# Projections of an adaLN and infini-attention block: x transposed ahead of the kernel, modulation columns on VectorE, and memory in groups of seven heads

## The chip, the cores and the metric

The kernel runs on one core of a Trainium2 chip. The metric is the device time of one execution in microseconds (us). Of the kernel before there are three timed runs, of 1843.55, 1843.55 and 1844.84 us, median 1843.55 us, and one more run that was profiled.

A core has four compute engines with a list of instructions each: TensorE (PE in the profile, its weight loads are PEld), VectorE (DVE), ScalarE (ACT) and GpSimd (POOL). SyncE (SP) issues most DMAs, in the order of its list. Matrix products go to PSUM banks of 128 x 512 floats; everything else lives in SBUF tiles of 128 partitions or in DRAM.

## The reference

One token stream of 2048 tokens and 576 features goes through an attention block and a feed-forward block, both with a modulated layer norm. The attention works on four segments of 512 tokens with 32 heads of 18, and carries a linear memory from segment to segment.

```python
mod = (silu(c) @ w_mod).reshape(1, 6, 1, 576)
sa, ca, ga, sb, cb, gb = (mod[:, i] for i in range(6))
h = layernorm(x) * (1 + ca) + sa
q, k, v = h @ wq, h @ wk, h @ wv                # 32 heads of 18, 4 segments of 512
phi = lambda t: where(t > 0, t + 1, exp(t))
for s in range(4):                              # M and z start at 0
    a_dot = softmax(qs @ ks.T * scale + causal) @ vs
    a_mem = (phi(qs) @ M) / (phi(qs) @ z + 1e-6)
    o_s = sigmoid(beta) * a_mem + (1 - sigmoid(beta)) * a_dot
    M, z = M + phi(ks).T @ vs, z + phi(ks).sum(tokens)
x = x + ga * (o @ wo)
h = layernorm(x) * (1 + cb) + sb
x = x + gb * ((silu(h @ w_gate) * (h @ w_up)) @ w_down)
```

## The kernel before

All products are done at about float32 precision: an operand is split into a rounded high part and a remainder, and a product takes three matmuls (high by high, low by high, high by low). So each operand comes as a pair: hh and hl for the normalised x, wqkh and wqkl for the weights of q and k, fh and fl for a projected tile.

**Projections, 0 to 242 us.** `wk1`, `ps1` and other pools hold this stage, in which the scheduler of the tile framework orders the instructions of each engine by what they depend on and by the order of the code. A loop runs over the four segments s. In each, `proj(s, t)` makes nine tiles of 128 features x 512 tokens (t 0 to 4 hold k, 4 to 8 hold q), each by 14 matmuls of 512 columns (tile pp); `vproj(s, i)` makes v for four groups of 128 tokens, two halves of 14 matmuls with 288 columns (pv); `phi_k` transposes a k tile (ptk) and forms phi(k) (pk); and `mem(s)` multiplies pk with v into five memory tiles (pm), which VectorE masks into mbd and GpSimd adds to the segment before. Results are stored to DRAM by SyncE: kD and qD hold three rows a feature (high, high, low for k, and high, low, high for q), since the scores are later made from stacks of these rows.

The input of a segment is made by `prep` and `trans_in`. `prep(s + 1)` loads x, takes mean and variance on VectorE and normalises it there. `trans_in(s + 1)` then lets TensorE transpose it, five groups of four 128 x 128 transposes (tile pt), and ScalarE and VectorE scale, shift and split each group into hh and hl. The groups stand at the end of a segment, between the last pv matmuls and the memory tiles: the border.

The modulation vectors: those of the first layer norm are made at the start (tiles wm, pr, row, pcr, colv). The four others follow in `late_mod`, from segment 1 on: products of w_mod rows with silu(c) are summed on VectorE (macc), and summed over partitions by TensorE, either into rows for the two gates (`mod_row`) or into columns for the second layer norm (`mod_col`: 20 matmuls of one column each, twice).

PSUM has eight banks. In this stage three belong to pp and pv, two to pt and ptk (tag t), one to memory and modulation (tag m), and two to scores (tag s1). `early()` runs the first pass of the first two attention units during the segments 1 to 3: scores s and their row maxima, `E1` steps a projection tile and `E2` steps a pv group.

**Attention, 242 to 613 us.** Here the order is written out by hand. There are 32 units of four heads of one segment, each in 11 steps. `PAT` names the events of each step by letters: among them A0, A1 and B0, B1, C (num, phi(q) by memory, in two halves, its copies and its division), M0 to M3 and X (output projection of attention: pw, from oh and ol), R, S, T, Z (its transposes of o), m and n (row maxima transposed), and g, h (phi of q). `RL` sets the steps of another stream, which prepares the feed-forward input.

**Feed-forward, 613 us to the end**, follows and is not changed.

Memory before: head groups of 128 feature rows don't fall on head limits (18 rows a head), so `mem` and `num_a` take one tile of 76 columns and four of 152 (eight heads with 19 columns each), the heads at the limits stand in two tiles, and `num_c` adds the halves. 

Of the kernel before, what the change touches and what calls it, by code (L numbers as in the profile page):

```python
# [15 lines left out]
P = 128  # L16
S = 2048
# [14 lines left out]
MB = [0, 3, 10, 17, 24]  # L32
MO = [0, 76, 228, 380, 532]
# [29 lines left out]
E1 = 3  # L63
E2 = 2
BK = 0
PAT = (["E", "", "U D", "m c", "n G", "Q d", "M0", "g M1 M2 M3 X", "h A0", "R S q T Y Z B0", "A1 f P z B1 C"],
# [3 lines left out]
LNA = 1  # L70
RB = 9
RL = (-6, -1, 0, 4, 4, 10, 11, 11, 13, 11, 12, 13, 16, 17)
# [9 lines left out]
def block(ctx: ExitStack, tc: tile.TileContext, x, wqk, wv, wo, beta, wgu, wgr, wd, c, w_mod, w_mod0, w_mod1, out):  # L82
# [8 lines left out]
    def chain(*g):  # L91
        for a in g:
            yield from a

# [57 lines left out]
    kD = [dr.tile([D, 3, L], F32, tag=f"kD{s}", name=f"kD{s}") for s in range(NSEG)]  # L152
# [3 lines left out]
    xhD = [dr.tile([P, 4, D], F32, tag=f"xh{s}", name=f"xh{s}") for s in range(NSEG)]  # L156
    xD = [dr.tile([P, 4, D], F32, tag=f"xD{s}", name=f"xD{s}") for s in range(NSEG)]
# [6 lines left out]
    mbd = vst.tile([P, 3, 5, 152], F32, tag="mbd", name="mbd")  # L164
# [4 lines left out]
    SB = [2]  # L169

    def load_stack(u, b):
        s, q = units[u]
        k, v = [d[s].rearrange("f z t -> (f z) t").rearrange("(Q a r) t -> Q r a t", Q=8, a=2)[q] for d in (kD, qD)]
        for r0, r1 in ((0, 96), (96, 108)):
            nc.sync.dma_start(f32(kst[b][r0:r1]), k[r0:r1])
        for r0, r1 in ((0, 48), (54, 102), (48, 54), (102, 108)):
            nc.sync.dma_start(f32(qst[b][r0:r1, r0 // 54:4:2, :]), v[r0:r1])
# [6 lines left out]
    def p1_step(u, b, i, ps, jp, jb):  # L184
# [18 lines left out]
        if i == 0:  # L203
            nc.gpsimd.tensor_scalar(mc[:, 0], mx, -1.0, 0.0, op0=ALU.mult, op1=ALU.add)
            lo = mwk.tile([P, 4, 4], F32, tag="ml", name="ml")
            nc.gpsimd.tensor_tensor(lo, mx, f32(mc[:, 0]), op=ALU.add)
            nc.gpsimd.tensor_scalar(mc[:, 1], lo, -1.0, 0.0, op0=ALU.mult, op1=ALU.add)
# [35 lines left out]
    def transpose_group(pt, src, kt):  # L243
        for i in range(4):
            n = P if kt < 4 else 64
            nc.tensor.transpose(pt[:n, 128 * i:128 * i + 128], src(i)[:, 128 * kt:128 * kt + n], ident)
# [10 lines left out]
    with ExitStack() as p1:  # L257
# [8 lines left out]
        def early():  # L266
            for u in range(2):
                load_stack(u, u)
            for u in range(NE):
                yield from p1_unit(u, u, ps, "m", 1, pb, 2)  # L270
# [6 lines left out]
        bdm = w1.tile([P, 5, 8, VW], F32, tag="bdm", name="bdm")  # L277
        nc.gpsimd.memset(bdm, 1.0)
        for t in range(5):
            off = 128 * t - 64 - DH * MB[t]  # L280
            nc.gpsimd.affine_select(out=bdm[:, t], in_=bdm[:, t], pattern=[[-DH, 8], [0, VW]], compare_op=ALU.is_ge,
                                    fill=0.0, base=off, channel_multiplier=1)
            nc.gpsimd.affine_select(out=bdm[:, t], in_=bdm[:, t], pattern=[[DH, 8], [0, VW]], compare_op=ALU.is_ge,
                                    fill=0.0, base=DH - 1 - off, channel_multiplier=-1)
# [6 lines left out]
        def load_x(s):  # L291
            t = xs[s] = x1.tile([P, 4, D], F32, tag="x", name=f"x{s}")
# [22 lines left out]
        def mod_col(a, slot, add):  # L315
            pc = ps.tile([P, L], F32, tag="m", name="pc", bufs=1)
            for c in range(6):
                c0 = 288 * (c // 3) + 128 * (c % 3)
                if c % 3 < 2:
                    nc.tensor.matmul(pc[:, c:c + 1], lhsT=a[:, c0:c0 + 128], rhs=ones[0:96, 0:1], start=True, stop=True)  # L320
# [1409 lines left out]
```

## Time and profile before

| what | us |
|---|---|
| median of the three timed runs | 1843.55 |
| the profiled execution's own time | 1842.27 |
| its span in the trace | 1840.5 |
| TensorE busy | 1806.1 |
| VectorE busy | 1488.5 |
| ScalarE busy | 1095.0 |
| GpSimd busy | 642.1 |
| 243 to 613 us: TensorE busy of 370 | 356.3 |
| 613 us to the end: TensorE busy of 1227.5 | 1221.2 |

The profile comes from one execution that the hardware profiler recorded. Its span leaves out 1.8 us around the recorded work. In rows of groups, "idle before" is what the engine waited ahead of these instructions, and the name behind the arrow is what ended most of it. In rows of the timeline, the first number is the start and the second the length; TensorE overlaps its instructions, so a length is more than the distance to the next start. A matmul on 32-bit data shows as two instructions.

### The profile page before, as it was taken

What the parts mean: (1) busy time and instruction counts of PE and PEld (TensorE: products, weight loads), DVE (VectorE), ACT (ScalarE), POOL (GpSimd) and SP (SyncE); (2) the same over time, 40 slices, a digit from 0 to 9 for tenths busy, and PEclk for the clock granted to TensorE, in tenths of its full rate; (3) what the DMA queues carried; (4) which work ended last, traced back from release to release, by engine and by line L of the source; (5) the groups of instructions that cost most, each with busy time, mean ns of one, the idle gap of its engine ahead of it and who ended that gap; (6) DMA issues with size and microseconds to landing.
All of it is one profiled execution on the core that took longest, in us unless ns stands there. A gap on an engine that the chain in (4) does not pass through costs nothing.

```text
span 1840.5 us, 31635 instructions
## 1 busy us (share of the span) xinstructions
PE 1806.1 (98%) x10727; PEld 1535.0 (83%) x10727; DVE 1488.5 (81%) x3361; ACT 1095.0 (59%) x2380; POOL 642.1 (35%) x1118
## 2 busy tenths in 40 slices
PE   7999999999999999999999999999999999999999
PEld 4888866787776888888888888898888888888888
DVE  7455358878886799898898899868888888888886
ACT  3333468878776567777777777634454544544541
POOL 5000058776556575565665665400000000000000
PEclk9999999999999999999999999999999999999999
DMA  7767677778674845555545545485332333334331
GB/s 262 226 229 258 234 208 193 201 203 210 177 183 145 289 145 188 162 160 174 161 156 177 147 135 160 153 292 169 128 106 84 122 106 111 102 100 128 106 101 53
DMA packets 149417, 305.56 MB, mean 166 GB/s; under 512 B 30057, under 2 KB 60905, under 8 KB 147337
## 3 DMA queue, kind: packets, MB, share of 16 engines
q1 hardware_dynamic: 138360, 259.20, 48.0%
q10 hardware_dynamic: 10896, 44.36, 6.2%
q8 instruction: 85, 1.39, 0.3%
q14 instruction: 76, 0.61, 0.1%
HBM read 193.29 MB, written 109.64 MB: 165 GB/s over the span
## 4 chain that ended last, share of the span: by engine, by line
PE 90%; DVE 3%; DMA 3%; ACT 2%; POOL 1%; issue 1%; SPq 0%; ACTq 0%; POOLq 0%; DVEq 0%
PE A L1258 25%; PE pd L1377 19%; PE C L1258 12%; PE B L1258 6%; PE pp L108 5%; PE av L651 4%; PE s L194 3%; PE pv L108 3%; PE pw L761 3%; PE s L627 3%; PE pd L1397 3%; DVE junk L199 1%; ACT Pt L634 1%; PE pm L458 1%; PE pn L832 1%
## 5 line engine op out<-in xcount | busy, mean ns | idle before, releaser
L1258 PE MATMUL A<-y,wh 128*128 128x512 f32 x1152 | 404.2, 391 | 2.5 <-ACT B L1304 1.8
L1385 DVE TENSOR_TENSOR acc<-acc,pd 128x576 f32<-128x576 f32 x327 | 245.4, 751 | 77.2 <-PE pd L1377 71.4
L199 DVE CUSTOM_DVE_ANT_0 junk<-s,tri 128x256 bf16<-128x256 f32 (+3 forms) x512 | 221.8, 484 | 64.9 <-PE s L194 49.7
L1377 PE MATMUL pd<-dh,ah 128*128 128x288 f32 x896 | 267.4, 298 | 0.1
L1377 PE MATMUL pd<-dl,ah 128*128 128x288 f32 x896 | 263.8, 294 | 0.0
L1377 PE MATMUL pd<-dh,al 128*128 128x288 f32 x896 | 262.4, 293 | 0.0
L1258 PEld LDWEIGHTS A<-y,wh 128*128 128x128 f32 x1152 | 216.2, 188 | 41.3 <-ACT B L1304 2.1
L1220 DVE TENSOR_TENSOR wl<-O,wh 128x256 fp32r<-128x256 f32 x504 | 241.9, 483 | 3.5 <-ACT wh L1219 2.9
L1258 PE MATMUL A<-y,wl 128*128 128x512 f32 x576 | 224.6, 390 | 0.0
L634 ACT ACTIVATE Pt<-s 128x512 f32<-128x512 f32 (+1 forms) x352 | 181.6, 559 | 48.2 <-PE s L627 28.3
L1258 PE MATMUL C<-y,wh 128*128 128x512 f32 x576 | 202.7, 393 | 0.0
L1219 ACT CAST wh<-O 128x256 fp32r<-128x256 f32 x504 | 198.2, 405 | 2.8 <-DMA O<-in_wgu_dram 1.5
L1377 PEld LDWEIGHTS pd<-dh,ah 128*128 128x128 f32 x896 | 168.1, 188 | 19.0 <-ACT pd L1353 4.1
L1323 DVE TENSOR_TENSOR al<-sg,ah 128x512 fp32r<-128x512 f32 x240 | 178.3, 743 | 6.6 <-ACT ah L1322 6.5
L1377 PEld LDWEIGHTS pd<-dl,ah 128*128 128x128 f32 x896 | 169.5, 189 | 16.2
L1213 POOL TENSOR_TENSOR O<-O 128x128 f32<-128x128 f32 x280 | 155.4, 588 | 64.7 <-DMA O<-in_wgu_dram 27.7
L1377 PEld LDWEIGHTS pd<-dh,al 128*128 128x128 f32 x896 | 169.1, 189 | 0.0
L1322 ACT CAST ah<-sg 128x512 fp32r<-128x512 f32 x240 | 149.2, 621 | 26.3 <-DVE sg L1282 24.8
L627 PE MATMUL s<-qs,ks 110*128 110x512 f32 (+2 forms) x384 | 143.8, 392 | 5.3 <-ACT Pt L634 4.1
L194 PE MATMUL s<-ks,qs 108*128 108x256 f32 (+3 forms) x512 | 144.3, 334 | 2.1 <-DVE mx L199 1.9
L1258 PEld LDWEIGHTS C<-y,wh 128*128 128x128 f32 x576 | 108.0, 188 | 18.8
L1258 PEld LDWEIGHTS A<-y,wl 128*128 128x128 f32 x576 | 108.2, 188 | 14.8
(377 smaller groups left out, 4084.5 us busy)
## 6 DMA issues: line engine op xcount, KB each, us to landing
wr<-rD SPq DMA_DIRECT2D x216, 112.0 KB
O<-in_wgu_dram SPq DMA_DIRECT2D x36, 512.0 KB
oD<-O ACTq DMA_DIRECT2D x36, 512.0 KB
O<-oD SPq DMA_DIRECT2D x36, 512.0 KB
O<-in_wgu_dram SPq DMA_DIRECT2D x36, 384.0 KB
ks<-kD SPq DMA_DIRECT2D x32, 384.0 KB
qs<-qD SPq DMA_DIRECT2D x64, 192.0 KB
y<-yD SPq DMA_DIRECT2D x11, 1024.0 KB
```

The costliest lines, as they stand in the source:

```text
L194: nc.tensor.matmul(bank[:, n * (h - h0):n * (h - h0) + n], lhsT=qst[b][0:108, h, 128 * i:128 * i + 128], rhs=kst[b][0:108, h // 2, 0:n], s ...
L199: nc.vector.tensor_tensor_reduce(junk[:, :n], bank[:, n * (h - h0):n * (h - h0) + n], tri[:, L - n:], 1.0, -3e38, op0=ALU.add, op1=ALU.max ...
L627: nc.tensor.matmul(bank[:, n * (g - h):n * (g - h + w)].rearrange("p (a b) -> p a b", a=w), lhsT=kst[u % NB][0:110, g // 2, 128 * j:128 * ...
L634: nc.scalar.activation(pt[:, h:h + per, :n], bank[:, :n * per].rearrange("p (a b) -> p a b", a=per), AF.Exp, scale=SCALE)
L1213: eng.tensor_tensor(o[:, d, i, s_], o[:, a, i, s_], o[:, b, i, s_], op=op)
L1219: nc.scalar.copy(wh, o)
L1220: later.append(lambda: nc.vector.tensor_tensor(wl, o, f32(wh), op=ALU.subtract))
L1258: nc.tensor.matmul(bank, lhsT=a, rhs=b, start=(first and n == 0), stop=(n == 6), skip_group_check=not first)
L1322: nc.scalar.copy(ah, src)
L1323: later.append(lambda: nc.vector.tensor_tensor(al, src, f32(ah), op=ALU.subtract))
L1377: nc.tensor.matmul(pd[:, i, :288], lhsT=a[:, tk], rhs=w, start=(add and k == 0), stop=(k == 2), skip_group_check=not add)
L1385: nc.vector.tensor_tensor(o, o, pd[:, :, :288], op=ALU.add)
```

## The change

- **x transposed.** The host also passes x transposed (`xt`). For the segments 1 to 3, `prep` loads it as five tiles of 128 features x 512 tokens, and loads the rows of x as well, only for mean and variance. GpSimd forms the reciprocal deviation; mean and deviation go to DRAM (sD) and come back broadcast to all partitions (two tiles rw). GpSimd then subtracts, multiplies and scales each tile, and `cast_in` at the border casts it on ScalarE (hh) and subtracts on VectorE (hl). Segment 0 keeps its transposes.
- **Modulation columns on VectorE.** `mod_col` goes. Nine products with a sum, of 128 x 576, take its place on VectorE, with silu(c) broadcast to all partitions (srow, a reciprocal of 128 x 576 among its steps). `late_mod` starts in segment 2 instead of late in segment 1.
- **Seven-head memory groups.** Memory tiles hold seven heads, 126 rows and 133 columns, four times, and one of four heads, 72 x 76. No head stands in two tiles, and `num_c` adds nothing. The tag m goes: memory and `mod_row` use the two banks of tag t, pr and pcr those of s1.
- **Three store buffers.** fh and fl become one tile with three buffers; kD holds high and low once; a k tile is stored by one DMA instead of two, and the stack of k is loaded by three DMAs, the high row twice.
- **A fixed first order.** The matmuls of pr, the first two groups of pt and pcr are pinned to the order of the code.
- **A third bank for first-pass scores**, with two `early` steps a projection tile and one a pv group instead of three and two. The small steps that end a first pass move from GpSimd to VectorE for the first two units.
- wv's high part is cast on ScalarE instead of GpSimd, and a few events of `PAT` and `RL` stand a step earlier.

```diff
-E1 = 3
-E2 = 2
+E1 = 2
+E2 = 1
-       ["U E", "", "D m", "n", "G c", "d", "M0 M1 M2 M3 X Q g h", "R S", "q A0 B0 T", "Z Y", "P f z A1 B1 C"],
-       ["D E", "U m l", "n G p", "M0", "M1 M2 M3 X A0", "B0", "x c", "d", "", "A1 Q g", "B1 q Y h C P f"])
+       ["U E", "", "D m", "n", "G c", "M0 d", "M1 M2 M3 X Q g h", "R S T", "A0 B0", "q Z Y", "P f z A1 B1 C"],
+       ["D E", "U m l n", "G p", "M0 M1", "M2 M3 X", "A0", "x c B0", "d", "", "A1 Q g", "B1 q Y h C P f"])
...
-    SB = [2]
+    SB = [3]
...
         def late_mod():
+            pk_ = [("r", 2, k) for k in range(6)] + [("c", n) for n in range(9)] + [("r", 5, k) for k in range(6)]
...
+            nc.scalar.activation(se, srow, AF.Exp, scale=-1.0)
+            nc.vector.tensor_scalar(se, se, 1.0, None, op0=ALU.add)
+            nc.vector.reciprocal(se, se)
+            nc.vector.tensor_tensor(srow, srow, se, op=ALU.mult)
...
+                    nc.vector.tensor_tensor_reduce(t, t, srow, 1.0, 1.0 if b < 4 else 0.0, op0=ALU.mult, op1=ALU.add,
+                                                   accum_out=d)
...
+        def cast_in(s):
+            hh, hl, hr = new_h(s)
+            for kt in range(5):
...
+                    nc.scalar.copy(hh[kt], f)
+                    nc.vector.tensor_tensor(hl[kt], f, f32(hh[kt]), op=ALU.subtract)
...
         def prep(s):
+            load(0)
+            load(1)
+            nc.sync.dma_start(t[:, 0:4], xt[0:512, L * s:L * s + L].rearrange("(k p) t -> p k t", p=P))
+            nc.sync.dma_start(t[0:64, 4], xt[512:576, L * s:L * s + L])
...
+            nc.gpsimd.tensor_tensor(mr[:, 1], mr[:, 1], mhalf[:, :4], op=ALU.pow)
+            nc.sync.dma_start(sD[s].rearrange("z (p i) -> p z i", i=4), mr)
+            for z in range(2):
+                nc.sync.dma_start(rw[z], sD[s][z].partition_broadcast(P))
...
+            for kt in range(5):
+                n = P if kt < 4 else 64
+                f = t[:n, kt]
+                nc.gpsimd.tensor_tensor(f, f, rw[0][:n], op=ALU.subtract)
+                nc.gpsimd.tensor_tensor(f, f, rw[1][:n], op=ALU.mult)
+                nc.gpsimd.tensor_scalar(f, f, colv[:n, kt, 0:1], colv[:n, kt, 1:2], op0=ALU.mult, op1=ALU.add)
...
         def mem(s):
             for t in range(5):
-                nh = 4 if t == 0 else 8
-                n = nh * VW
-                pm = ps.tile([P, L], F32, tag="m", name="pm", bufs=1)
+                n, r = NH[t] * VW, NH[t] * DH
+                pm = ps.tile([P, L], F32, tag="t", name="pm")
                 for i in range(4):
-                    nc.tensor.matmul(pm[:, :n], lhsT=pk[:, i, 128 * t:128 * t + 128],
-                                     rhs=vs[s][:, i, VW * MB[t]:VW * MB[t] + n], start=(i == 0), stop=(i == 3))
+                    nc.tensor.matmul(pm[:r, :n], lhsT=pk[:, i, PR * t:PR * t + r],
+                                     rhs=vs[s][:, i, 7 * VW * t:7 * VW * t + n], start=(i == 0), stop=(i == 3))
...
+            fb = pb.tile([P, 2, L], F32R, tag="fh", name="fh", bufs=3)
...
-            tg = trans_in(s + 1) if s + 1 < NSEG else iter(())
             for i in range(4):
...
-                if i == 2:
-                    next(tg, None)
+            tg = cast_in(s + 1) if s + 1 < NSEG else iter(())
             next(tg, None)
             if s < 3:
                 for _ in mem(s):
                     next(tg, None)
```

Three places of the program show how instructions move. First, TensorE's list at the border between segments 0 and 1, before; pv, pm and pp are the tiles named above, pt a transpose group, s a first-pass score:

```order
L108 MATMUL pv<-wvl,hr 128x288
L246 MATMUL pt<-ident,x_603 128x128 x4
L458 MATMUL pm<-vs_728,pk 128x76 x4
L246 MATMUL pt<-ident,x_603 128x128 x4
L458 MATMUL pm<-vs_728,pk 128x152 x4
L108 MATMUL pp<-hh_827,wqkh 128x512
L108 MATMUL pp<-hh_827,wqkl 128x512
L108 MATMUL pp<-hl_831,wqkh 128x512
L458 MATMUL pm<-vs_728,pk 128x152 x4
```

The same place with the change:

```order
L113 MATMUL pv<-wvl,hr 128x288
L534 MATMUL pm<-vs_732,pk 126x133 x16
L534 MATMUL pm<-vs_732,pk 72x76 x4
L113 MATMUL pp<-hh_864,wqkh 128x512
L113 MATMUL pp<-hh_864,wqkl 128x512
L113 MATMUL pp<-hl_868,wqkh 128x512
```

The transposes are gone, and the five memory tiles, which were spread among transposes and the first matmuls of the next segment, stand in one run right behind the last pv. 

Second, the start of TensorE's list, before (pr sums the modulation of the first layer norm, pt transposes segment 0's x, pcr turns the row into columns):

```order
L371 MATMUL pr<-wm_252,sgb 32x320 x4
L246 MATMUL pt<-ident,x_248 128x128 x4
L371 MATMUL pr<-wm_255,sgb 32x320 x4
L246 MATMUL pt<-ident,x_248 128x128
L371 MATMUL pr<-wm_258,sgb 32x320 x4
L246 MATMUL pt<-ident,x_248 128x128 x3
L378 MATMUL pcr<-ident,row 128x128 x2
L378 MATMUL pcr<-ident,row 64x128
L475 MATMUL pp<-hh_354,wqkh 128x512
```

The same place with the change:

```order
L373 MATMUL pr<-wm_248,sgb 32x320 x4
L255 MATMUL pt<-ident,x_244 128x128 x4
L373 MATMUL pr<-wm_251,sgb 32x320 x4
L373 MATMUL pr<-wm_254,sgb 32x320 x4
L380 MATMUL pcr<-ident,row 128x128 x2
L380 MATMUL pcr<-ident,row 64x128
L255 MATMUL pt<-ident,x_244 128x128 x4
L551 MATMUL pp<-hh_359,wqkh 128x512
```

Both lists have eight transposes here. Before, the first four belonged to the first two groups, two each, and took the x tiles that were ready first; now they are the whole first group, ahead of the last two parts of pr, and the second group stands behind pcr. 

Third, SyncE's list in segment 0, from the last k stores on, before (wvraw are the loads of wv, x those of the next segment):

```order
L497 DMA kD_94<-fh 64x2x512
L498 DMA kD_94<-fl 64x512
L503 DMA qD_90<-fh 64x2x512
L504 DMA qD_90<-fl 64x512
L539 DMA wvraw<-in_wv_dram 128x576
L295 DMA x_603<-in_x_dram 128x576 x2
L503 DMA qD_90<-fh 128x2x512
```

The same place with the change:

```order
L572 DMA kD_94<-fh 128x1024
L504 DMA sD_125<-mr 128x2x4
L577 DMA qD_90<-fh 64x512
L572 DMA kD_94<-fh 64x1024
L506 DMA rw<-sD_125 128x512 x2
L576 DMA qD_90<-fh 64x1024
L612 DMA wvraw<-in_wv_dram 128x576 x2
L576 DMA qD_90<-fh 128x1024
```

The loads of the next x have moved ahead of this piece, the store of mean and deviation and its two broadcast loads have come in, and two loads of wv, instead of one, now stand here, behind them.

More of the change, by code (lines that the diff above doesn't have):

```diff
@@ L93, in chain, with once @@
             yield from a
+    def once(g):
+        yield next(g)
     def run(g):
@@ L269, in early @@
             for u in range(NE):
-                yield from p1_unit(u, u, ps, "m", 1, pb, 2)
+                yield from p1_unit(u, u, ps, "t", 2, pb, 2)
             load_stack(2, 2)
@@ L539, in load_wv @@
                 nc.sync.dma_start(r, wv[:, k, :])
-                split(wvh[:, k], wvl[:, k], r)
+                nc.scalar.copy(wvh[:, k], r)
+                nc.vector.tensor_tensor(wvl[:, k], r, f32(wvh[:, k]), op=ALU.subtract)
                 yield
@@ L593, in block @@
                     next(tg, None)
-            for _ in tg:
-                pass
+            run(tg)
         run(ge)
```

287 lines of the change are left out of this document (157 added, 130 removed).

## Prediction

> **What bounds the kernel now.** I read the page's busy times first, then its chain, then the busy time by stretches, and only then single rows.
>
> ```profile
> PE 1806.1 (98%) x10727; PEld 1535.0 (83%) x10727; DVE 1488.5 (81%) x3361; ACT 1095.0 (59%) x2380; POOL 642.1 (35%) x1118
> PE 90%; DVE 3%; DMA 3%; ACT 2%; POOL 1%; issue 1%; SPq 0%; ACTq 0%; POOLq 0%; DVEq 0%
> ```
>
> TensorE is busy for 98% of 1840.5 us and holds 90% of the chain that ended last. So an edit is worth what it takes off TensorE's own list, plus or minus the gaps it closes or opens. The change touches the projections (0 to 242 us) and the attention behind them; here are the stretches, with segment borders apart.
>
> ```profile
> 0.00:30.00 30.00, 17.49 (x94) 9.48 (x95) 22.54 (x46) 9.03 (x14) 20.60 (x43) 1.00 0.71 239
> 30.00:74.00 44.00, 42.75 (x251) 37.09 (x251) 23.13 (x45) 16.45 (x31) 5.95 (x7) 1.00 0.82 261
> 141.00:189.00 48.00, 47.73 (x283) 41.33 (x281) 25.73 (x53) 17.51 (x36) 1.57 (x4) 1.00 0.76 253
> 189.00:199.00 10.00, 10.00 (x69) 9.05 (x68) 5.27 (x11) 5.64 (x9) 2.49 (x4) 1.00 0.42 151
> 246.00:300.00 54.00, 48.94 (x344) 32.32 (x343) 41.93 (x180) 44.63 (x100) 42.57 (x73) 0.94 0.71 189
> ```
>
> The first number after the length is TensorE's busy time. At the border behind segment 2 (189 to 199) it has no gap at all, and inside segment 2 (141 to 189) a quarter of a microsecond. Whatever leaves TensorE's list there is gained in full, unless a new wait replaces it. Only the start and the first attention units (246 to 300, 5 us idle, clock 0.94) leave something to win by better timing.
>
> **Part 1, the transposes of x and the seven-head memory groups.** TensorE around the border between segments 0 and 1 (start, length, instruction):
>
> ```profile
> 67.66 0.60 PE L246 MATMUL pt<-ident,x 128*128 128x128 f32 x4
> 68.02 0.38 PE L108 MATMUL pv<-wvh,hh 128*128 128x288 f32 x1
> ...
> 71.83 0.60 PE L246 MATMUL pt<-ident,x 128*128 128x128 f32 x4
> 72.27 1.01 PE L458 MATMUL pm<-vs,pk 128*128 128x76 f32 x8
> 73.12 0.60 PE L246 MATMUL pt<-ident,x 128*128 128x128 f32 x4
> ...
> 75.45 1.20 PE L458 MATMUL pm<-vs,pk 128*128 128x152 f32 x8
> 76.38 0.73 PE L194 MATMUL s<-ks,qs 108*128 108x512 f32 x2
> 76.95 0.40 PE L108 MATMUL pp<-hh,wqkh 128*128 128x512 f32 x1
> ...
> 81.77 0.39 PE L108 MATMUL pp<-hh,wqkl 128*128 128x512 f32 x1
> 82.00 0.40 PE L108 MATMUL pp<-hl,wqkh 128*128 128x512 f32 x1
> ```
>
> Lengths overlap, so I count from start to start. A projection matmul takes 0.23 us (82.00 less 81.77), a transpose group 0.44 (72.27 less 71.83), a 152-column memory tile 0.93 (76.38 less 75.45; its four calls show as eight instructions) and the 76-column one 0.85. From 71.83 to 82.00 there are 12 projection matmuls (2.80) and two score matmuls (76.38 to 76.95, 0.57); the remaining 10.17 - 2.80 - 0.57 = 6.80 us are five memory tiles, four transpose groups and the switches between them. Afterwards four tiles of 133 columns (0.91 each, between 0.85 and 0.93) and one of 76 stand there in one run: 4 x 0.91 + 0.85 = 4.5, with 0.2 for a switch 4.7. That saves 2.1; the fifth group, inside the pv matmuls, gives another 0.36 (68.02 less 67.66). So 2.5 a border and **-7.6 us** for three.
>
> What is late next at a border? The new hh and hl tiles. They were paced by ScalarE's two evacuations a tile; now one cast and one subtraction do.
>
> ```profile
> L255 DVE TENSOR_TENSOR hl<-hf,hh 128x512 fp32r<-128x512 f32 x16 | 11.9, 751 | 21.0 <-ACT hf L254 21.0
> L461 DVE TENSOR_TENSOR mbd<-pm,bdm 128x152 f32<-128x152 f32 (+1 forms) x15 | 4.5, 301 | 13.2 <-PE pm L458 13.2
> L490 ACT CAST fh<-pp 128x512 fp32r<-128x512 f32 x36 | 21.2, 588 | 22.7 <-PE pp L108 16.8 <-DMA qD<-fh 4.2 <-ACT pe L448 0.9
> ```
>
> VectorE's 21.0 us of idle ahead of hl show that pace. ScalarE's work per border falls from ten evacuations to five casts of 0.59 (the fh row, the same size). VectorE keeps five subtractions of 0.75 and five mask products of 0.30, 5.3 us against 4.5 of memory tiles and 2.8 of the first projection tile: it fits, but a memory tile reuses a bank whose product can stand behind a subtraction. That can hold TensorE for 0 to 1 us a border, at most one subtraction and the hand-over; I take 0.3, so **+0.9** (0 to 3). The Trainium skill, SBUF — State Buffer, section Who interferes with whom, says that a VectorE instruction with both inputs in SBUF contends with a GpSimd instruction reading SBUF; hl is such a one. That would make the subtractions slower while GpSimd adds memory tiles. The rows of before can't tell: the hl rows never met such work in this number. By the rule the sum would be up to 1 us worse a border behind segments 1 and 2, which the bounds hold.
>
> **The preparation on GpSimd.** A segment now needs ten 128x512 products and five 128x512 scalings there.
>
> ```profile
> L820 POOL TENSOR_TENSOR pq<-qe,qf 128x512 f32<-128x512 f32 (+1 forms) x15 | 19.3, 1284 | 1.2 <-ACT qf L812 0.8
> L88 POOL TENSOR_SCALAR wvh<-wvraw 128x576 fp32r<-128x576 f32 x5 | 4.1, 822 | 18.2 <-DMA wvraw<-in_wv_dram 18.2
> 46.14 1.02 SPq L539 DMA_DIRECT2D wvraw<-in_wv_dram x1
> 50.95 0.68 POOL L88 TENSOR_SCALAR wvh<-wvraw 128x576 fp32r<-128x576 f32 x1 [13.97 <-DMA wvraw<-in_wv_dram]
> 56.06 0.30 PE L108 MATMUL pv<-wvh,hh 128*128 128x288 f32 x1
> ```
>
> 10 x 1.28 + 5 x 0.82 = 16.9 us, beside a GpSimd that is 5.95 busy of 44 in segment 0 and 1.57 of 48 in segment 2: hidden, if its inputs arrive 17 us ahead of the border. In segments 1 and 2 they do: statistics are asked for at the first tiles. Segment 0 is tight. The mean and rstd go to DRAM and come back broadcast (sD, two rw loads), and SyncE issues in order: the last two wv loads now stand behind that round trip. Before, the last was issued at 46.14, was picked up at 50.95 and was wanted from 56.06 on. The sD store's landing, taken like that load's at up to 4.8 us, moves the issue to 49 to 51 (an estimate from these rows), the pick-up to 54 to 56 and the end of cast and subtraction (0.6 and 0.75) to 55 to 57: about in time, but ScalarE and VectorE have fh and fl of the last tiles in front. GpSimd then ends near 53 + 17 = 70, the border being at 71.8. I take **+1.0** (0 to 2.5, if the landing is 2 to 3 us later than that). The bytes hardly change: x is read twice and rw adds 0.5 MB, while kD keeps two rows instead of three.
>
> **Part 2, modulation columns on VectorE.** What TensorE loses:
>
> ```profile
> 167.80 0.50 PE L320 MATMUL pc<-ones,macc 96*128 96x1 f32 x4
> ...
> 169.10 0.50 PE L108 MATMUL pp<-hh,wqkh 128*128 128x512 f32 x1
> L313 DVE SCALAR_TENSOR_TENSOR macc<-wml,sg,macc 96x576 f32<-96x576 f32 x20 | 16.1, 807 | 11.8 <-DMA wml<-in_w_mod_dram 11.7
> 7.91 0.35 DVE L357 RECIPROCAL gat<-gat 128x32 f32<-128x32 f32 x1
> ```
>
> A burst lasts 169.10 - 167.80 = 1.3 us and there are two: **-2.6**. VectorE gets nine products of 128x576 for twelve macc steps (0.81 each), and a reciprocal of 576 columns: 32 columns take 0.35 us, so at most 11 ns each and 6 us in all; at the 0.81 of a macc step it would be the other end, and I take 3. In 141 to 189 VectorE is 25.7 busy of 48, and this hides it; if it met a border, the price would be up to 6 us, once.
>
> **Part 3, the start.**
>
> ```profile
> 16.73 1.14 PE L371 MATMUL pr<-wm,sgb 128*32 128x320 f32 x8
> 17.80 0.55 PE L246 MATMUL pt<-ident,x 128*128 128x128 f32 x3
> 20.29 0.47 PE L475 MATMUL pp<-hh,wqkh 128*128 128x512 f32 x1 [1.16 <-ACT hh L253]
> ```
>
> The pinned order wants all four normalised x tiles before the last two pr groups. Two pr groups of 1.07 each (17.80 less 16.73) then follow it, and the chain row, pcr, colv, hh as before. The trace shows only that the fourth tile was there at 17.80. If it is ready by 15.7, pr ends at 17.8 as before and nothing is lost; if at 16.9, just ahead of its place of before, 1.2 is. I take **+0.5** (0 to 1.2).
>
> **Part 4, attention.** 96 of the 120 num instructions shrink from 152 to 133 columns, 0.02 us for eight: **-0.3**. Three store buffers remove ScalarE's 4.2 us of waiting for qD stores (the fh row); TensorE is 42.75 busy of 44 in segment 0 all the same, so at most 1 us could come of it, and I take nothing. Fewer GpSimd steps in num_c and a third score bank can shorten the waits of units 0 to 5. How much hangs on the clock:
>
> ```profile
> 266.00:270.00 4.00, 2.10 (x17) 1.45 (x21) 3.52 (x20) 3.27 (x7) 4.00 (x5) 1.00 0.66 158
> 270.00:274.00 4.00, 4.00 (x35) 1.83 (x28) 0.38 (x5) 1.28 (x3) 1.73 (x5) 0.57 0.87 229
> ```
>
> After 4 us half idle the granted clock is 0.57 for the next 4, so that 4.0 busy us hold 2.3 us of work: 1.7 lost. The mean clock of 0.94 over 246 to 300 stands for 54 x 0.06 = 3.2 us, so there are about two such drops. The Trainium skill, TensorE: Matmul & The Clock Gate, section What's actually happening, states that the clock is halved after an idle window of about 3.4 us and given back after a busy one; the trace agrees in the length of the loss, but here half idleness was enough. I take **-1** for attention, between -5 (both drops and their idle gone) and +3 (one drop and a wait more).
>
> **The sum**: -7.6 + 0.9 + 1.0 - 2.6 + 0.5 - 0.3 - 1.0 = -9.1. The profiled run took 1842.27 us (1840.5 and 1.8 around it), so 1833.2; the median of three, 1843.55, lies 1.3 above it, and on that scale the forecast is **1834.4**. A measurement tells 0.2%, 3.7 us, from no change.
>
> **Rivals.**
> - *The borders give it back.* Memory tiles wait for mask products behind subtractions, or hh for GpSimd's last scaling: 2 us at each border, and the wv stall at its 2.5. Sum -9.1 + 5 + 1.5 = -2.6: 1841. For it: two banks, and VectorE full for 5.3 us there. Against it: the products had one bank before, behind the same subtractions, and the border row shows no idle.
> - *The event tables bring waits* (slower). M0, the first output-projection matmul of a tile, and others move one step earlier: a step is 370 / 363 = 1.0 us, and 12 units have the M0 move. If their inputs come a step later than wanted, 12 x 1.0 us, with one drop of 1.7, turn -9.1 into +4.6: 1848. It decides from a lateness of 0.8 us a unit. Against it:
>
> ```profile
> 396.35 0.69 DVE L745 TENSOR_TENSOR ol<-pto,oh 128x512 fp32r<-128x512 f32 x1
> 402.35 0.30 PE L761 MATMUL pw<-woh,oh 128*128 128x288 f32 x1
> ```
>
> the later of its two inputs was ready 402.35 - 397.04 = 5.3 us ahead in this unit, five steps.
> - *Both clock drops go*, with the idle before them (1.9 in 266 to 270): -9.1 - 4 = -13: 1830.
> - *The scheduler hides no more than before*, the transposes having been free: 0. Against it: no idle at the borders.
>
> **How the numbers follow.** Forecast, -6 to -12: 0.55. Clock drops gone: 0.15. Borders give it back: 0.17. Nothing changes: 0.05. Tables: 0.08. Faster than 1839.9: all of the forecast and the clock case, and a little of the first rival, 0.72; within 0.2%: 0.20; slower: 0.08. The range goes from 1826 (clock case with no new waits) to 1844 (first rival with the bounds of segment 0).
>
> **What would show it.** Right: borders where memory tiles stand in one run of 4.5 us with no pt; no pc with 96x1; the first segment's pv starting by 57. Wrong: idle of TensorE before pm released by mbd, or before the first pp of a segment released by hh; pv waiting for wvl in segment 0; new granted clocks under 1 behind 242 us.

## The result, and the profile after

The changed kernel takes 1835.15 us (median of four runs, 1833.84 to 1836.13) against 1844.19 us before: a ratio of 0.995, 95% interval 0.9932 to 0.9967, 9.0 us less. The forecast was 1834.4 us, 9.1 less. Three terms under that sum were wrong, in both directions, and one wait was not in it; the sections below are mostly about these.

The page of the changed kernel, its busy times and the head of its chain:

```profile
PE 1796.2 (98%) x10627; PEld 1524.9 (83%) x10627; DVE 1488.8 (81%) x3371; ACT 1085.5 (59%) x2371; POOL 676.5 (37%) x1104
PE 93%; ACT 2%; DMA 2%; DVE 1%; issue 1%; POOL 1%; SPq 1%; ACTq 0%; DVEq 0%; POOLq 0%
```

TensorE's list is 9.9 us shorter (1806.1 to 1796.2) and still 98% of the span; GpSimd has taken 34 us more work. The starts of the same points of the program in the timelines of three executions (us; "again" is a second execution of the changed kernel, the first run below) show where the time went:

| point of the program | before | changed | changed, again |
|---|---|---|---|
| first matmul of pr | 9.46 | 10.47 | 8.71 |
| first projection matmul | 20.29 | 24.66 | 22.91 |
| segment 0: first pv | 56.06 | 59.36 | 57.85 |
| border 0, behind the last pv | 71.83 | 74.20 | 72.69 |
| segment 1: first pv | 115.92 | 117.10 | 115.42 |
| border 1 | 131.45 | 132.69 | 131.01 |
| segment 2: first pv | 173.04 | 170.84 | 169.15 |
| border 2 | 188.81 | 186.02 | 184.76 |
| segment 3: first pv | 226.16 | 219.96 | 218.71 |
| first attention products | 249.65 | 243.05 | 241.80 |
| first feed-forward matmul | 610.87 | 604.06 | 601.70 |
| end of the span | 1840.5 | 1834.4 | 1833.3 |

At the start 2.6 to 4.4 us are lost. From the first projection matmul to the first attention products the changed kernel then gains 10.5 to 11 us; attention is within 1.3 us, and the feed-forward part, which is the same program, came out 0.7 and 2.0 us longer in these two executions. That much is the spread of single executions, so stages are compared by their own starts. For the same reason the three spans differ by 6.1 and 7.2 us and not by the 9.0 of the medians: the profiled execution of before (1842.27 us) was faster than each of its four timed runs.

**The borders.** TensorE's timeline at border 0 (start, length, instruction):

```profile
74.07 0.29 PE L113 MATMUL pv<-wvl,hr 128*128 128x288 f32 x1
74.20 4.32 PE L534 MATMUL pm<-vs,pk 128*126 128x133 f32 x40
78.32 0.48 PE L113 MATMUL pp<-hh,wqkh 128*128 128x512 f32 x1
```

All five memory tiles stand in one run of 4.12 us, and the next segment's hh is ready at its end. At the other two borders one projection matmul stands between the memory tiles. The groups of the weight load and of the mask product over all three borders:

```profile
L534 PEld LDWEIGHTS pm<-vs,pk 128*126 128x126 f32 (+1 forms) x120 | 13.0, 179 | 0.5 <-DVE mbd L537 0.5
L537 DVE TENSOR_TENSOR mbd<-pm,bdm 126x133 f32<-126x133 f32 (+1 forms) x15 | 4.1, 279 | 2.0 <-PE pm L534 1.9
```

The wait for mask products, the loss that was feared there, is 0.5 us in all, and none of it is idle time of the matmuls.

**Segment 0.** The round trip of mean and deviation, SyncE's and GpSimd's rows, and the first pv:

```profile
46.37 0.38 SPq L504 DMA_DIRECT2D sD<-mr  x1
48.21 1.24 SPq L506 DMA_DIRECT2D rw<-sD  x2
50.00 1.41 SPq L612 DMA_DIRECT2D wvraw<-in_wv_dram  x2
53.41 2.54 POOL L513 TENSOR_TENSOR x<-x,rw 128x512 f32<-128x512 f32 x2 [5.79 <-DMA rw<-sD]
70.30 0.77 POOL L515 TENSOR_SCALAR x<-x,colv 64x512 f32<-64x512 f32 x1
59.36 0.30 PE L113 MATMUL pv<-wvh,hh 128*128 128x288 f32 x1
```

The wv loads are issued at 50.00, the first pv waits for nothing, and GpSimd needs 17.7 us (53.41 to 71.07) and is done 3.1 us ahead of the border.

**The start.** TensorE, VectorE and GpSimd in the first 25 us:

```profile
14.09 0.81 PE L255 MATMUL pt<-ident,x 128*128 128x128 f32 x2 [0.19 <-DVE x L250]
17.11 0.33 PE L255 MATMUL pt<-ident,x 128*128 128x128 f32 x1 [2.21 <-DVE x L250]
19.12 0.48 PE L255 MATMUL pt<-ident,x 128*128 128x128 f32 x1 [1.68 <-DVE x L250]
24.66 0.76 PE L551 MATMUL pp<-hh,wqkh 128*128 128x512 f32 x1 [0.30 <-ACT hh L262]
11.57 2.94 DVE L250 TENSOR_SCALAR x<-x,mv,rs 128x576 f32<-128x576 f32 x2
15.56 1.50 DVE L250 TENSOR_SCALAR x<-x,mv,rs 128x576 f32<-128x576 f32 x1
11.87 1.84 POOL L141 MEMSET qs<- 128x1024 f32 x2
15.47 0.95 POOL L141 MEMSET qs<- 128x1024 f32 x1
```

VectorE's same four steps before:

```profile
13.09 1.34 DVE L241 TENSOR_SCALAR x<-x,mv,rs 128x576 f32<-128x576 f32 x2
15.66 1.45 DVE L241 TENSOR_SCALAR x<-x,mv,rs 128x576 f32<-128x576 f32 x2 [0.36 <-POOL rs L237]
```

TensorE stands twice for the third and the fourth normalised x tile. VectorE's steps, about 0.7 each before (1.34 and 1.45 for two), take 1.5 here for the first three: the third starts at 15.56, GpSimd's memset runs to 16.42, and the step ends 0.64 behind it. And the first projection matmuls run at half the clock, which the windows show:

```profile
18.00:28.00 10.00, 7.87 (x34) 4.88 (x35) 6.68 (x12) 4.15 (x7) 4.73 (x7) 0.50 0.35 111
```

**Segment 1.** One new wait of TensorE stands there, for VectorE's half of a projected tile:

```profile
107.81 0.50 PE L113 MATMUL pp<-hh,wqkh 128*128 128x512 f32 x1 [1.34 <-DVE fh L567]
```

### The profile page after: what moved, and what is told of

Same layout as the page of the kernel before. It is cut to its first block, busy times and chain, and to the rows that moved or that the text cites. A ratio compares the mean times of both kernels' runs of the same rounds, so it can differ in the third digit from the quotient of the medians.

```text
span 1834.4 us, 31434 instructions
## 1 busy us (share of the span) xinstructions
PE 1796.2 (98%) x10627; PEld 1524.9 (83%) x10627; DVE 1488.8 (81%) x3371; ACT 1085.5 (59%) x2371; POOL 676.5 (37%) x1104
## 4 chain that ended last, share of the span: by engine, by line
PE 93%; ACT 2%; DMA 2%; DVE 1%; issue 1%; POOL 1%; SPq 1%; ACTq 0%; DVEq 0%; POOLq 0%
PE A L1309 25%; PE pd L1428 19%; PE C L1309 12%; PE B L1309 6%; PE pp L113 6%; PE av L720 4%; PE s L202 4%; PE s L696 3%; PE pv L113 3%; PE pw L830 3%; PE pd L1448 3%; ACT Pt L703 1%; PE pm L534 1%; PE pn L898 1%; PE px L741 1%
```

## Experiments

Twelve kernels ran, each timed against the kernel before on the same chip. Ratios are to that kernel; a difference of 0.001 is 1.8 us.

| run | ratio | 95% interval |
|---|---|---|
| changed kernel again | 0.9951 | 0.9937 to 0.9966 |
| no fixed order | 0.9946 | 0.9932 to 0.9959 |
| early memsets | 0.9933 | 0.9919 to 0.9948 |
| both of these | 0.9929 | 0.9913 to 0.9945 |
| columns on TensorE, started in segment 2 | 0.9996 | 0.9986 to 1.0006 |
| columns on TensorE, started in segment 1 | 0.9962 | 0.9950 to 0.9974 |
| transposes on TensorE | 0.9985 | 0.9976 to 0.9995 |
| two score banks and the thick spread | 1.0044 | 1.0029 to 1.0059 |
| two score banks alone | 0.9956 | 0.9941 to 0.9972 |
| thick spread alone | 1.0036 | 1.0022 to 1.0049 |
| old event tables | 0.9961 | 0.9948 to 0.9973 |
| no fixed order, early memsets, maxima on GpSimd | 0.9918 | 0.9902 to 0.9935 |

### Why the start is late

The theory at first was that the fixed order makes TensorE wait; rivals were late x data in that one execution, and slow normalising steps whatever the order. The changed kernel ran again, unaltered:

> The changed kernel once more, unaltered. Question: is its late start (first projection matmul at 24.66 us against 20.29 before) a property of the order, or of one execution in which the x tiles landed late (VectorE's first statistics at 7.94 against 6.21)? Theory order: the first projection matmul comes at 24 to 25 again, with two gaps of TensorE before the third and fourth transpose of about 2 us each. Rival late data: statistics start near 6.2, and the first projection matmul comes at 21 to 22. The median should lie 9 us under the kernel before (0.995).

Statistics started at 6.19 this time, not 7.94, and the first projection matmul still came at 22.91, behind two gaps of 2.07 and 1.68 us. So late data explains 1.75 of the 4.4 us of the first execution, and the gaps are a property of the kernel: the result lies between what the theory and its rival gave. Then the fixed order was taken away:

```diff
-            pin = tc.keep_in_program_order
+            pin = lambda i: i
```

> The changed kernel without the fixed first order: the scheduler places pr, the first transposes and pcr. Theory order: pr no longer waits for the x tiles, so pcr follows at about 19 and the first projection matmul comes at 20.3 to 21.5, 3 to 4 us earlier than with the fixed order; the clock stays at 1.00 in 18 to 28; the whole is 3 to 4 us faster than the changed kernel. Rival (the normalising steps are slow, whatever the order): the first projection matmul comes no earlier than 23, and the whole moves less than 1 us.

Measured: the ratio hardly moves (0.9946), and the first projection matmul comes later, not earlier.

```profile
23.56 0.77 PE L551 MATMUL pp<-hh,wqkh 128*128 128x512 f32 x1 [1.16 <-ACT hh L262]
24.12 0.63 PE L551 MATMUL pp<-hh,wqkl 128*128 128x512 f32 x1
24.55 0.63 PE L551 MATMUL pp<-hh,wqkh 128*128 128x512 f32 x1
```

The theory that the order alone is at fault falls: left to itself, the scheduler also puts transposes of late tiles between the pr groups. The next run kept the order and moved GpSimd's memsets to its first instructions, where it waits for nothing:

```diff
...
+    def stack_tiles(b, stk):
+        qst[b] = stk.tile([P, 4, L], F32R, tag=f"qs{b}", name=f"qs{b}")
+        kst[b] = stk.tile([P, 2, L], F32R, tag=f"ks{b}", name=f"ks{b}")
+        nc.vector.memset(f32(qst[b][:, 0:2]), 0.0)
+        nc.gpsimd.memset(f32(qst[b][:, 2:4]), 0.0)
+
+    for b in range(3):
+        stack_tiles(b, sk)
...
```

> The changed kernel with the fixed order kept, but GpSimd's three memsets of the score stacks (128x1024) moved from 11.9-16.4 us to its first instructions, so that nothing long runs on GpSimd while VectorE normalises x. Theory contention (VectorE's normalising step takes 1.4 to 1.5 us beside a GpSimd memset, against 0.65 without): the four steps take 0.65 to 0.7 each, the fourth transpose stands at 15.5 to 16.5 instead of 19.12, the first projection matmul at 21 to 22, and the whole is about 3 us faster. Rival (order or late data alone): the steps still take 1.4 us, or the fourth transpose stays behind 18, and the whole moves less than 1 us.

The normalising steps, all four in one group, with the memsets beside them (the changed kernel, first line) and without (this run, second line):

```profile
L250 DVE TENSOR_SCALAR x<-x,mv,rs 128x576 f32<-128x576 f32 x4 | 5.4, 1373 | 0.7 <-POOL rs L246 0.7
```

```profile
L257 DVE TENSOR_SCALAR x<-x,mv,rs 128x576 f32<-128x576 f32 x4 | 2.2, 574 | 0.7 <-POOL rs L253 0.6
```

1373 ns (1164 in the repeat of the changed kernel) against 574: the contention is shown. The move also gave VectorE's list another order, with the statistics of the fourth tile ahead of all normalising steps, so the lengths are the contention's alone and the earlier starts come from both. The fourth transpose moves to 16.77 (15.5 to 16.5 was expected) and the first pv of segment 0 to 56.45, although pr itself began 0.7 us later than in the repeat of the changed kernel; the ratio is 0.9933, 3.3 us better than the changed kernel's, as expected, though with intervals that overlap. The projection matmul still starts only at 22.31, later than expected, since the fixed order keeps two pr groups and pcr behind that transpose. Both edits together:

> Both edits: no fixed order and early memsets. If order and contention are two halves of one loss (either alone removes most of it), this is at most 1 us faster than the better of the two: first projection matmul at 19.5 to 20.5, the whole 3.5 to 5 us faster than the changed kernel, 0.992 to 0.993 of the kernel before. If they add up instead, it is 6 us faster or more.

```profile
20.39 0.77 PE L558 MATMUL pp<-hh,wqkh 128*128 128x512 f32 x1 [1.16 <-ACT hh L269]
```

This row of the run with both lies near that of before (20.29 there), though pr began 1.0 us earlier in this execution, and the ratio is 0.9929. Counted from the first matmul of pr, which takes out how early an execution's first data came, the first pv of segment 0 stands 46.60 us behind it before, 48.89 and 49.14 in the two executions of the changed kernel, 50.25 without the fixed order, 47.01 with early memsets and 46.60 with both. Once the x tiles come in time, the fixed order costs about 0.9 us at the first projection matmul (22.31 less 20.39, less the 1.0 by which pr began later in the run with early memsets) and 0.4 at the first pv; while they come late, it costs nothing. The two are not halves of one loss: contention comes first, and the order matters only behind it. The times alone don't separate these kernels: the four intervals overlap.

### What the parts of the gain are worth

The transposes were put back on TensorE, and the seven-head memory groups kept:

```diff
-            tg = cast_in(s + 1) if s + 1 < NSEG else iter(())
+            tg = trans_in(s + 1) if s + 1 < NSEG else iter(())
...
         def prep(s):
+            run(load_x(s))
+            yield
+            mv, rs = ln_stats(wk, [xs[s][:, i, :] for i in range(4)], 4)
+            yield
+            for i in range(4):
+                xhat(xs[s][:, i, :], xs[s][:, i, :], mv, rs, i)
...
```

> The changed kernel with the x of segments 1 to 3 normalised on VectorE and transposed on TensorE again, memory groups of seven heads kept. Theory sum: five groups at 0.36 to 0.44 us a border, 2.1 a border, so 6.3 us slower than the changed kernel over the three borders, the store of mean and deviation and GpSimd's 17 us gone. Memory tiles and transposes now share two banks, which can add up to 1 us a border. Rival (the memory groups, not the transposes, brought the border's gain): under 2 us slower.

The ratio goes from 0.9951 to 0.9985, 6.3 us as expected. The three stretches from the last pv of a segment to the first pv of the next grow by 1.8, 4.6 and 1.7 us (42.73, 38.14, 33.95 in the repeat of the changed kernel; 44.53, 42.78, 35.64 here), 8.1 in this execution. So the transposes, with the way that x takes to avoid them, are most of the borders' gain. The memory groups were not run alone, so their share is only what is left over.

The modulation columns went back to TensorE twice: once with `late_mod` starting in segment 2, as the change has it, and once starting late in segment 1, as before.

```diff
+                elif p == 4:
+                    mod_col(a, 0, 1.0)
+                elif p == 3:
+                    mod_col(a, 1, 0.0)
...
-                if s > 1:
+                if s > 1 or s == 1 and t > 4:
```

> The changed kernel with the modulation columns of the second layer norm made by TensorE again (two bursts of 20 one-column matmuls), all else as changed. Theory sum (the bursts are worth their 1.3 us each): the segments 2 and 3 of the projections take 2.6 us longer together (2.2 to 3.0 from the first projection matmul behind border 2 to the first attention products), and the whole is about 2.6 us slower than the changed kernel. Rival (VectorE's products or its reciprocal cost as much in another place): the difference is under 1 us.

> The modulation columns on TensorE again, with their steps starting late in segment 1 as before the change (the run that started them in segment 2 was 7.3 us slower, 2.4 of it in the segments and the rest in the first attention units). Theory sum: 2.6 us slower than the changed kernel, all of it in the projections, the first attention units as in the changed kernel to within a clock drop (1.7 us). Rival (the bursts collide with the new order of the segments): 5 us slower or more again.

The second of them gives 0.9962, 2.0 us slower than the changed kernel, near the 2.6 expected, but with ten runs spread over 9.8 us and an interval that overlaps the changed kernel's, so the time alone doesn't show a loss. In its profiled execution, one of the two slowest of the ten, a burst takes about 1.3 us, as before, and two new waits stand beside the bursts:

```profile
PE pv L113 <- ACT pf L568: 2.0, 1, 2.0
PE pp L113 <- DVE fh L566: 1.9, 1, 1.9
```

The first gives 0.9996, 8.3 us slower, which neither its theory (2.6) nor its rival (under 1) had. In its profiled execution the two stretches that hold the bursts, from the first pv of segment 2 to border 2 and on to the first pv of segment 3, are 2.9 us longer than in the repeat of the changed kernel (17.34 and 35.16 against 15.61 and 33.95), and the rest up to the first feed-forward matmul is 5.4 us longer, with a mean granted clock over 236 to 330 us of 0.91 instead of 0.98. Started in segment 2, the last of the twenty-four steps on VectorE begins at 225.7 us (196.7 in the repeat), and the second gate's row is summed at 236.9, behind the last pv (226.6 in the repeat, 8 us ahead of it), so attention begins beside it. That this is what slows the first attention units isn't shown. The change has 21 such steps and started as late; that the later start and the columns on VectorE belong together was not seen ahead.

### The spread of the early first pass

> The changed kernel with two banks for first-pass scores and three and two steps of the early first pass, as before the change. Theory sum: worth nothing within 1 us at the end of the projections, since TensorE had no gap there. Rival (the third bank and the thinner spread earn part of the gain in segments 1 and 2): the stretch from border 0 to border 2 becomes 2 us longer or more, by waits of TensorE for VectorE's row maxima.

This was meant as a small undoing and is the largest effect of the study: 1.0044, 17 us slower than the changed kernel and slower than before. The two halves apart:

```diff
-    SB = [3]
+    SB = [2]
...
```

> The changed kernel with two banks for first-pass scores, the thin spread (two and one steps) kept. The run before with both undone lost 14.5 us in segment 2, where SyncE's list stood still from 145 to 162 us behind a load of x rows that waited for VectorE's statistics. Theory spread (three steps a tile put the rest of the early work, and the reciprocal, ahead of those statistics): the bank alone is worth under 1.5 us, mostly short waits for row maxima in segment 1. Theory bank (two banks hold TensorE): 10 us or more slower than the changed kernel.

```diff
-E1 = 2
-E2 = 1
+E1 = 3
+E2 = 2
```

> The changed kernel with three banks, but three and two steps of the early first pass a tile. Theory spread: segment 2 loses 8 to 15 us, with TensorE waiting for fh (VectorE) and pf (ScalarE) and SyncE standing still ahead of a kD store, as with both undone. Theory bank: within 1.5 us of the changed kernel. If both this and the bank alone cost little, the loss needs both.

The bank alone is worth nothing that can be measured (0.9956); the spread alone is all of it (1.0036). TensorE's longest waits in the projections with the thick spread:

```profile
PE pp L113 <- DVE fh L567: 7.4, 1, 7.4
PE pv L113 <- ACT pf L569: 4.2, 1, 4.2
```

Its SyncE and VectorE rows in segment 2 (start, length, instruction) say why:

```profile
144.17 1.37 SPq L482 DMA_DIRECT2D xb<-in_x_dram  x2
145.64 1.02 SPq L485 DMA_DIRECT2D x<-in_xt_dram  x1
146.71 1.36 SPq L486 DMA_DIRECT2D x<-in_xt_dram  x1
163.19 0.33 SPq L482 DMA_DIRECT2D xb<-in_x_dram  x1
...
165.61 0.43 SPq L572 DMA_DIRECT2D kD<-fh  x1
158.07 3.75 DVE L410 RECIPROCAL se<-se 128x576 f32<-128x576 f32 x1
161.74 0.40 DVE L493 BATCH_NORM_STATS2 st<-xb 128x6 f32<-128x288 f32 x1
166.55 0.80 PE L113 MATMUL pp<-hh,wqkh 128*128 128x512 f32 x1 [7.41 <-DVE fh L567]
```

SyncE issues nothing from 148 to 163 us. The third load of x rows waits for a buffer that VectorE's statistics must free, and on VectorE's list those stand behind the reciprocal, which the scheduler has put behind four tiles of segment 2. The kD stores of those tiles are behind that load on SyncE's list, so the three fh buffers fill and TensorE stops. In the changed kernel (the repeat) the same instructions stand one tile into the segment:

```profile
137.62 3.75 DVE L410 RECIPROCAL se<-se 128x576 f32<-128x576 f32 x1
143.84 1.77 SPq L482 DMA_DIRECT2D xb<-in_x_dram  x2
```

and nothing stops. So two numbers of the change that look like tuning are what lets its other parts work: with the old spread, the new preparation of x and the three buffers lose 16 us.

### The event tables

```diff
...
-       ["U E", "", "D m", "n", "G c", "M0 d", "M1 M2 M3 X Q g h", "R S T", "A0 B0", "q Z Y", "P f z A1 B1 C"],
+       ["U E", "", "D m", "n", "G c", "d", "M0 M1 M2 M3 X Q g h", "R S", "q A0 B0 T", "Z Y", "P f z A1 B1 C"],
...
-RL = (-6, -1, 0, 4, 4, 9, 10, 10, 12, 10, 11, 12, 15, 16)
+RL = (-6, -1, 0, 4, 4, 10, 11, 11, 13, 11, 12, 13, 16, 17)
```

> The changed kernel with the event tables of before (PAT and RL). Theory: the attention stretch (first attention products to the first feed-forward matmul) stays within 1.5 us of the changed kernel's 361, since no moved event was waited for. Rival (the moved events pay for, or cost, attention time): it changes by 3 us or more, either way; the wait of scores for the row maxima's DMA, 4.4 us in the changed kernel and 1.0 before, would shrink if the tables brought it.

0.9961, with an interval that holds the changed kernel's. From the first attention products to the first feed-forward matmul this execution took 359.55 us (242.90 to 602.45), the changed kernel 361.01 and 359.90. No sign of an effect either way. One wait in this stage did grow with the change, that of scores for the row maxima's DMA (us in all, times, longest; before and the repeat):

```profile
PE s L627 <- DMA qs<-mr: 1.0, 2, 0.7
PE s L696 <- DMA qs<-mr: 4.6, 2, 2.8
```

With the old tables it is still 3.5, so they aren't its cause; what is was not tried.

### A faster version

```diff
-            eng = nc.vector if u < NE else nc.gpsimd
+            eng = nc.gpsimd
...
-        for i in range(3):
+        for i in range(6):
```

> A try for a faster version: no fixed order and early memsets (0.9929 of the kernel before), and in addition the small steps that end a first pass back on GpSimd, with the transposition of the maxima three steps later. VectorE spent 2.05 us on these three steps in segment 1 (103.35 to 105.4), in front of two subtractions that TensorE waited for, 1.2 to 1.4 us. Expected: that wait goes, 1 to 1.4 us faster than without this edit, about 1829.5. Rival (GpSimd, busy preparing x, ends the maxima so late that TensorE waits for their transposition): 0 to 3 us slower.

On top of early memsets and no fixed order, this gives 0.9918 (0.9902 to 0.9935), an interval that lies below that of the changed kernel's repeat: it beats both kernels, by 15 and by about 6 us. TensorE's wait for fh in segment 1 is gone from its waits, and its projections ended 3.1 us earlier than without this edit (228.96 against 232.09), 0.7 of it already at the first pv of segment 0. In that execution, the slowest of its six, attention gave back more than this: from the last pv to the first feed-forward matmul it took 6.3 us longer, at a mean clock of 0.93 over 236 to 330 us against 0.98. So whether the last edit itself pays isn't settled: the intervals of 0.9918 and 0.9929 overlap widely.

## Why the prediction came out as it did

- **What bounds the kernel, and the method.** Right: what left TensorE's list was gained, less the new waits. From the first pv of segment 0 to the last pv the two executions gain 9.3 and 9.1 us; the borders' 8.7 (next point) and the columns' 2.6, less the 1.9 of waiting in segment 1, are 9.4.
- **The borders, -7.6 and +0.9.** The mechanism was right, the size too small. The memory run takes 4.12 us, not 4.7, so with the fifth group the gain at border 0 is 6.80 + 0.36 - 4.12 = 3.0 instead of 2.5. Counted in the same way, the other two borders give 2.8 each. The feared waits for mask products came to nothing that stops a matmul: -8.7 in place of -6.7.
- **Segment 0, +1.0.** The first pv waits for nothing: 0. GpSimd took 17.7 us where 16.9 was given. That wv was issued at 50.00, where 49 to 51 was given, is luck, since the whole segment was late by then: counted back from the first pv, the issue stands 9.4 us ahead in both executions (50.00 to 59.36, 48.47 to 57.85) against 9.9 before (46.14 to 56.06). So the round trip moved it by 0.5 us and not by 3 to 5; the store of sD and the loads of rw are issued only 1.84 us apart (46.37 and 48.21), where up to 4.8 was taken.
- **Modulation columns, -2.6.** Undoing them cost 2.9 us in the stretches concerned in one form, and 2.0 us of time in the other, which is not clear of noise; a burst took 1.3 us again. So the size is right by the rows, while the times alone don't show it. VectorE's reciprocal took 3.75 us, where 3 was taken and 6 was the bound.
- **The start, +0.5 (0 to 1.2).** This is the step that failed: 2.6 and 4.4 us at the first projection matmul, 1.8 and 3.3 at the first pv (2.3 and 2.5 when counted from the first matmul of pr). The sum asked only when the fourth x tile had been ready before and took its readiness as unchanged. Even that could have been read: the second VectorE row of before, shown with the start above, ends at 17.11 us, and two pr groups of 1.07 behind it end at 19.25, which by the prediction's own reckoning costs 1.4 and lies above its bound. On top of it, GpSimd's memsets and small reciprocals fell in another order against VectorE's steps, and these stretched from 698 ns on average to 1373 and 1164 in the two executions. Why the scheduler chose this order isn't shown; GpSimd's early list is shorter with the change (bdm in one group), and VectorE's first normalising step now stands ahead of all of the fourth tile's statistics. The rule on SBUF that the prediction cited for hl, from the Trainium skill, SBUF — State Buffer, section Who interferes with whom, is not the one at work here, though a neighbour of it: the same section counts the scalar form that normalises x among those that can lock the port shared with GpSimd for a whole instruction, and the rows above agree (the step that began at 15.56 ended 0.64 us behind the memset). At the borders, where the cited rule was feared, hl took 686 ns.
- **Segment 1.** Not in the sum at all: 1.3 us of waiting for fh and 0.6 for row maxima. The first is contention too, now of two instructions with both inputs in SBUF, as was feared for hl. In the second execution of the changed kernel VectorE's three small steps behind a first pass, moved there from GpSimd, run beside GpSimd's preparation of x:

```profile
104.03 1.21 DVE L215 TENSOR_TENSOR ml<-mx,mc 128x16 f32<-128x16 f32 x1
102.68 2.52 POOL L514 TENSOR_TENSOR x<-x,rw 128x512 f32<-128x512 f32 x2
```

  1.21 us for 16 columns, ending at 105.24 as GpSimd's instruction ends at 105.19; the subtraction that TensorE waited for stood behind it. In the faster version above these steps are GpSimd's again, the same product takes 0.22 us there, and the wait is gone:

```profile
100.18 0.22 POOL L222 TENSOR_TENSOR ml<-mx,mc 128x16 f32<-128x16 f32 x1
```

- **Attention, -0.3 and -1.0.** From the last pv to the first feed-forward matmul, 0.8 less in one execution and 1.9 in the other: right in size. The cause stays open: the clock drops were not moved in a way that the change decides (see the last section), and the longer wait for the row maxima's DMA was not in the sum.
- **The rivals.** The tables bring no wait: shown by the run with the old ones. (They move M0 in six units and M1 in six others, not M0 in twelve.) The borders don't give the gain back. The slower side was looked for in the tables, and its real place was SyncE's list in segment 2, where the spread of the early first pass decides whether 16 us are lost; the change happens to stand on the good side.

So the sum came within 0.1 us of the measured difference because a border term too small by 2.0, and a segment 0 term too large by 1.0, met a start too cheap by 1.3 to 2.8 and a wait of 1.9 that wasn't foreseen. The two profiled executions themselves gain 6.8 and 9.2 us up to the first feed-forward matmul. The direction and the main mechanism were earned; that the sum came so close was luck.

## What to carry to other kernels

When an edit changes the order of the first instructions, look at what GpSimd now runs beside VectorE's steps, since here a step was twice as long beside it (1.2 to 1.4 us against 0.6). When work is taken off TensorE and its inputs come by a longer way (statistics, a store, a load back), follow the in-order DMA list through every stage, not only the one where slack is smallest. And undo the small numbers of a change one at a time: one of them may be what the large parts stand on.

## What the runs showed of the hardware that was not expected

The clock drops are not decided by the program alone. Windows of the same ten us in two executions of the changed kernel, the first with the row of the first execution, the second with that of the repeat (TensorE's busy time behind the length, the granted clock third from the end):

```profile
280.00:290.00 10.00, 8.50 (x55) 4.18 (x54) 4.63 (x23) 6.15 (x15) 8.62 (x15) 0.71 0.64 182
```

```profile
280.00:290.00 10.00, 8.11 (x59) 4.81 (x58) 6.21 (x29) 8.21 (x20) 9.19 (x15) 1.00 0.70 187
```

The one with more idle time kept its clock. A free-running window, as the Trainium skill has it in TensorE: Matmul & The Clock Gate, section What's actually happening, would allow that, since the same gap can fall inside one window or across two; the runs here don't show the window itself. And the granted clock isn't always on record: in the run without the fixed order the first projection matmuls stand 0.43 us apart (24.12 to 24.55), as at half the clock, where a later one takes 0.23, while this row of its windows gives 1.00:

```profile
24.00:26.00 2.00, 2.00 (x8) 1.62 (x8) 2.00 (x4) 1.42 (x3) 0.00 (x0) 1.00 0.70 216
```
